# Half-query blocks at both ends of a gated attention kernel, with a new head, lighter norm rows and a gate row read in order

## The chip, the cores and the metric

The kernel runs on one core of one Trainium2 chip. The metric is the device time of one execution in microseconds. Each execution also reports its span, from the first to the last instruction (1.7 to 2.1 us less than the time here), and the mean clock that the throttle granted TensorE. All executions compared below are of the fast state; three timed ones (one each of after_vd2, after_strided and after_gap2: 423.23, 431.38 and 424.83 us) fell in the slow state, at a clock of 0.956 to 0.967, and are left out.

## The reference, cut to what matters

```python
x = A_x                                                # 1 x 2048 x 448, bf16
g = sigmoid((x * gate_w).sum(-1, keepdims=True))
q, k, v = split(x @ wqkv)                              # 16 heads of 28
a = softmax(q @ k.T * 28**-0.5) @ v @ wo               # per head, 2048 x 2048 scores
b = irfft2(rfft2(x) * (w_r + 1j * w_i))                # over both axes
return g * a + (1 - g) * b
```

The attention needs 16 x 2048 x 2048 exponentials. The Fourier part is done with matmuls between the attention's own.

## The kernel before

The 16 heads are four groups of four. A *score* is one 128x512 tile: 128 keys against 512 queries of one head. Four query blocks in each of four head groups make 16 blocks of work, each with 16 key tiles of four heads: 1024 scores in all. ScalarE takes most of the exponentials, two or three scores per instruction, from PSUM banks psA (3) and psB (2) to a ring in SBUF. For one to three key tiles of each block (the list ND) VectorE does it instead: it evicts the four scores as integers (y) and makes four phases from them (pd); each phase is multiplied with its own scaled copy of the values (vd), which GpSimd makes. TensorE sums the products of both kinds in the bank pvb.

These are the parts that the argument touches. `pool`, `dve`, `pe` and `act` do not issue an instruction: they hand an operation to a list scheduler with an assumed duration, dependences and a key, and the instructions are emitted in the order that it finds. Here GpSimd's scaling is assumed to take 0.6 us:

```python
            self.vdops[g] = []
            for f in range(4):
                def fp(f=f):
                    self.pin(nc.gpsimd.tensor_scalar(out=self.vd[:, f, :, :, 0:DH + 1], in0=self.vf[:],
                                                     scalar1=PHGAIN[f], scalar2=None, op0=ALU.mult))
                self.vdops[g].append(self.pool(0.6, fp, [e2, pw, self.vdms], due))
            self.vdready[g] = self.vdops[g][-1]
            ...
        for g in range(1, 4):                       # vd is one buffer: the old products must be done
            for o in self.vdops[g]:
                o.deps += self.vdlast.get(g - 1, [])
```

The keys of all operations are then moved by a list of some three thousand offsets (KOFF) that an earlier tuning found. Where the scheduler counts a busy share of TensorE below HAMF over the last HAMW = 3.4 us, it adds *filler* products of zeros.

The gate row of the Fourier part goes through DRAM, so that all partitions get it, and is read in steps of 16 elements:

```python
        d = self.dma(self.escr[:], self.ge[:], (m,), due + 20.0, dur=0.6, lat=4.0)      # escr is [P, NT]
        ...
                                                 in1=free_dims(self.erow[0:FN], [[0, 4], [NT, P]], g),
                                                 op=ALU.mult))
```

Of the kernel before, what the change touches and what calls it, by code (L numbers as in the profile page):

```python
# [23 lines left out]
UNITS = 512.0  # L24
# [23 lines left out]
def fft_consts():  # L48
# [45 lines left out]
    for ri, B in enumerate((Br, Bi)):  # L94
# [8 lines left out]
       "selc": (386, 192), "sel8": (578, 128), "selw": (706, 4)}  # L103
CSTN = 710
# [10 lines left out]
def small_consts():  # L115
# [10 lines left out]
    selc = np.zeros((P, 4, 48))  # L126
    for s in range(4):
        sv[32 * s:32 * s + 2] = 1.0
        selq[32 * s + 2:32 * s + 30, 32 * s] = -0.5
        selk[32 * s + 2:32 * s + 30, 32 * s + 1] = -0.5  # L130
        for b in range(4):
            selc[32 * s + 2:32 * s + 30, b, 16 + 4 * s + b] = -0.5
# [3 lines left out]
    put("selc", selc.reshape(P, 192))  # L136
# [25 lines left out]
class Item:  # L162
# [6 lines left out]
HAMW, HAMF = 3.4, 0.7421  # L169
DUE_P = 6.757  # L170
PVK, DUW, DFREE, WREL = 6.037, 11.4211, 1, 13.243
GK, GQ, GW, GV, GS, GREL = 6.918, 2.841, 7.618, 6.073, 2.662, 35.075
PROT, PTOL = 1.7838, 0.0685
FD = 2.303
EXT, XM, MPEN = 0, 0.0773, 4.0862
PDK = 1.0
PTN, PTD = 6, 20.0
KOFF = (
    (0, -3381), (1, -3445), (2, -3205), (3, -2978), (4, -2807), (5, -3003), (6, -2741), (7, -3070), (8, -2870),
    (9, -2933), (10, -2699), (11, -2432), (12, -2665), (13, -2889), (14, -2827), (15, -2875), (16, -3046),  # L180
    (17, -2813), (18, -2716), (19, -2526), (20, -2725), (21, -2957), (22, -2530), (23, -2791), (24, -2754),
    (25, -2847), (26, -2318), (27, -2163), (28, -2008), (29, -2195), (30, -1969), (31, -2290), (32, -2267),
    (33, -2067), (34, -2601), (35, -3137), (36, -3254), (37, -3031), (38, -3281), (39, -3296), (40, -2974),
    (41, -2802), (42, -2682), (43, -2539), (44, -2686), (45, -2183), (46, -2186), (47, -2367), (48, -2465),
    (49, -2217), (50, -2391), (51, -2580), (52, -2825), (53, -2743), (54, -2507), (55, -2843), (56, -2900),
    (57, -3179), (58, -3134), (59, -3379), (60, -3643), (61, -3140), (62, -3042), (63, -3134), (64, -2754),
    (65, -2650), (66, -2451), (67, -2565), (68, -2390), (69, -2220), (70, -2100), (71, -2159), (72, -2061),
    (73, -2085), (74, -2080), (75, -1960), (76, -1798), (77, -1549), (78, -1626), (79, -1557), (80, -1441),
    (81, -1328), (82, -2731), (83, -2587), (84, -2436), (85, -2518), (86, -2456), (87, -2507), (88, -2279),
    (89, -2452), (90, -2493), (91, -2144), (92, -1906), (93, -1954), (94, -2137), (95, -1875), (96, -1981),  # L190
    (97, -1911), (98, -1824), (99, -1714), (100, -1653), (101, -1305), (102, -1132), (103, -1215), (104, -1487),
    (105, -1438), (106, -1094), (107, -1077), (108, -1034), (109, -1025), (110, -1166), (111, -1450), (112, -1274),
    (113, -1191), (114, -1077), (115, -1190), (116, -1417), (117, -1541), (118, -1613), (119, -1649), (120, -1257),
    (121, -1226), (122, -1283), (123, -1151), (124, -1121), (125, -1455), (126, -1620), (127, -2002), (128, -1724),
    (129, -1720), (130, -1658), (131, -1595), (132, -1435), (133, -1466), (134, -1247), (135, -1465), (136, -1097),
    (137, -1198), (138, -1426), (139, -1342), (140, -1235), (141, -1526), (142, -1267), (143, -944), (144, -1058),
    (145, -1130), (146, -813), (147, -777), (148, -958), (149, -843), (150, -1414), (151, -1407), (152, -1433),
    (153, -1322), (154, -1705), (155, -1737), (156, -1657), (157, -1437), (158, -1254), (159, -1349), (160, -1242),
    (161, -1169), (162, -1495), (163, -1374), (164, -1386), (165, -1347), (166, -1379), (167, -1189), (168, -1306),
    (169, -1092), (170, -1354), (171, -1386), (172, -1548), (173, -1534), (174, -1628), (175, -1488), (176, -1507),  # L200
    (177, -1437), (178, -1344), (179, -1580), (180, -1276), (181, -1067), (182, -1143), (183, -1519), (184, -1575),
    (185, -1316), (186, -2323), (187, -2506), (188, -2184), (189, -2238), (190, -2117), (191, -1965), (192, -1937),
    (193, -2420), (194, -1921), (195, -1458), (196, -1355), (197, -1502), (198, -1355), (199, -1162), (200, -1029),
    (201, -1030), (202, -817), (203, -897), (204, -722), (205, -800), (206, -975), (207, -1152), (208, -1016),
    (209, -774), (210, -872), (211, -919), (212, -910), (213, -1000), (214, -892), (215, -809), (216, -728),
    (217, -844), (218, -806), (219, -644), (220, -533), (221, -950), (222, -650), (223, -1130), (224, -1204),
# [278 lines left out]
TA, TB = 43.678, 14.609  # L485
OUTD = 15
XREL = 9.034
SWP = 1.8725


class Sched:
# [60 lines left out]
    def run(self, nbg_tiles, dunits, dfree):  # L552
# [76 lines left out]
        def finish(o, t0, dur):  # L629
            nonlocal left  # L630
            if o.eng == "PE":
                pebusy.append((t0, t0 + dur))
                if o.name == "pv":
# [5 lines left out]
                    if o.last:  # L639
                        pvopen[1] = o.step  # L640
# [11 lines left out]
        while left:  # L652
            progress = False
            for e in engs:
# [3 lines left out]
                for o in pend[e]:  # L658
# [26 lines left out]
                    if best is None or k < best[0]:  # L685
                        best = (k, o)
# [60 lines left out]
class Kernel:  # L747
# [15 lines left out]
    def build(self):  # L763
# [8 lines left out]
        for o in order:  # L772
            o.emit()
# [1205 lines left out]
```

## Time and profile before

| | |
|---|---|
| time, median of three timed runs | 421.18 us (420.97 to 422.19) |
| time and span of the profiled execution | 424.53 us, 422.8 us |
| its mean clock | 0.992 |
| scores on ScalarE | 856, steps 1.33 us for three and 0.90 for two |
| first exponential starts, last ends | 12.07, 410.46 |
| holes between exponentials, summed step by step | 16.5 us |
| tail after the last exponential | 12.34 us |

The row to remember is the second: the trace is of an execution 3.3 us slower than the median. In the time-line lines further down the columns are start, duration, engine, source line, operation, tiles and count, and in brackets how long the engine sat idle before and what released it. One line also belongs here, the change from head group 0 to 1:

```profile
124.05 4.83 POOL L1362 TENSOR_SCALAR vd<-vf 128x348 bf16<-128x348 f32 x4 [9.85 <-PE pvb L868]
...
132.91 0.40 PE L868 MATMUL pvb<-pd,vd 128*32 128x512 bf16 x4
```

GpSimd waits for the old group's products, makes the new values until 128.88, and the first product that uses them comes at 132.91 without any wait: there are four microseconds to spare.

### The profile page before, as it was taken

The page shows a single profiled execution, that of the slowest core. Times are in us where ns is not written, and L with a number is a line of the kernel's source. Part 1 is how long each engine was busy: PE and PEld are TensorE (multiplying, and loading weights), DVE is VectorE, ACT ScalarE, POOL GpSimd, SP SyncE. Part 2 cuts the span into 40 slices and gives each one's busy share as a digit, 9 for nine tenths or more (in the row PEclk, how much of TensorE's full clock was granted, in tenths as well). Part 3 has the DMA queues.
Part 4 walks back from the last instruction along what each step waited for, and adds up shares of the span by engine and source line. Part 5 has one row for each costly group of instructions (what it writes and reads, how often), then busy time and mean ns, then how long its engine had stood idle before and what let it go on. Part 6 is the DMA issues. An engine that isn't in the chain of part 4 may idle for free.

```text
span 422.8 us, 12521 instructions
## 1 busy us (share of the span) xinstructions
PE 396.1 (94%) x5319; PEld 151.2 (36%) x5319; DVE 369.0 (87%) x670; ACT 396.1 (94%) x362; POOL 32.9 (8%) x63
## 2 busy tenths in 40 slices
PE   6899899999999999999999999999989999999986
PEld 4443232323443323334333323443333333333334
DVE  5658698967889999998999999999998989998883
ACT  4889899999999999999999999999997999999981
POOL 5310300000021000000004000000021000000000
PEclk9999899999999999999999999999998999999999
DMA  8400010001122310110110100213211300000011
GB/s 247 113 2 3 3 25 18 3 2 52 43 68 50 96 52 2 44 46 2 43 42 10 35 4 12 102 46 95 80 32 35 101 3 13 12 25 25 24 47 44
DMA packets 26348, 17.96 MB, mean 42 GB/s; under 512 B 10632, under 2 KB 24756, under 8 KB 26292
## 3 DMA queue, kind: packets, MB, share of 16 engines
q1 hardware_dynamic: 25524, 16.88, 14.6%
q8 instruction: 41, 0.67, 0.7%
q10 hardware_dynamic: 768, 0.28, 0.3%
q14 instruction: 15, 0.12, 0.1%
HBM read 11.27 MB, written 1.84 MB: 31 GB/s over the span
## 4 chain that ended last, share of the span: by engine, by line
PE 41%; ACT 29%; DVE 13%; issue 11%; DMA 3%; POOL 2%; ACTq 0%; DVEq 0%; POOLq 0%
ACT ring L1498 29%; PE bg L868 18%; PE pvb L868 11%; PE psA L868 6%; PE psB L868 6%; DVE y L1456 4%; DVE pd L1466 3%; DVE xtok L1919 3%; POOL vd L1362 2%; DMA xtok<-in_A_x_dram 1%; DMA U<-Y 1%; DMA U<-in_A_wqkv_dram 1%; PE bg L877 0%; DVE Y L1837 0%; DVE t L1879 0%
## 5 line engine op out<-in xcount | busy, mean ns | idle before, releaser
L1498 ACT ACTIVATE ring<-psA 128x1536 bf16<-128x1536 f32 (+1 forms) x172 | 264.2, 1536 | 8.8 <-PE psA L868 6.6
L1498 ACT ACTIVATE ring<-psB 128x1024 bf16<-128x1024 f32 x171 | 191.8, 1122 | 0.8 <-PE bg L868 0.5
L1456 DVE TENSOR_SCALAR y<-bg 128x512 uint16<-128x512 f32 x168 | 112.8, 686 | 14.1 <-PE bg L868 13.0
L1466 DVE TENSOR_SCALAR pd<-y 128x2048 uint16<-128x2048 uint16 x168 | 112.3, 687 | 0.5
L868 PEld LDWEIGHTS <-k 32*128 32x128 bf16 (+1 forms) x1088 | 44.6, 91 | 125.6 <-issue 120.6
L868 PE MATMUL pvb<-ring,vw 128*32 128x512 bf16 x856 | 78.6, 389 | 0.0
L868 PE MATMUL psA<-q,k 32*128 32x512 bf16 x514 | 68.2, 385 | 9.0 <-ACT ring L1498 8.1
L868 PE MATMUL psB<-q,k 32*128 32x512 bf16 x342 | 68.4, 384 | 2.0 <-ACT ring L1498 1.5
L868 PE MATMUL pvb<-pd,vd 128*32 128x512 bf16 x672 | 60.2, 385 | 4.2 <-POOL vd L1362 2.9
L868 PE MATMUL bg<-q,k 32*128 32x512 bf16 x168 | 62.7, 385 | 0.5 <-DVE xtok L1919 0.2
L868 PEld LDWEIGHTS <-vw 128*32 128x32 bf16 x856 | 20.5, 95 | 30.5 <-issue 26.9
L868 PEld LDWEIGHTS <-vd 128*32 128x32 bf16 x672 | 16.9, 95 | 28.6 <-issue 19.0
L1362 POOL TENSOR_SCALAR vd<-vf 128x348 bf16<-128x348 f32 x16 | 19.1, 1195 | 89.0 <-PE pvb L868 85.2
L868 PEld LDWEIGHTS <-xT 128*128 128x128 bf16 (+3 forms) x512 | 18.9, 96 | 13.4 <-issue 11.5
L1837 DVE CAST Y<-bg 128x450 bf16<-128x450 f32 x32 | 19.6, 619 | 1.8 <-PE bg L868 0.8
L868 PE MATMUL bg<-X,R 128*32 128x225 bf16 (+1 forms) x384 | 20.0, 294 | 0.2 <-DVE y L1456 0.2
L868 PE MATMUL bg<-xT,wpq 128*32 128x512 bf16 (+1 forms) x240 | 18.9, 395 | 0.3
L868 PE MATMUL bg<-xT,wpk 128*32 128x512 bf16 (+2 forms) x244 | 18.8, 381 | 0.1
L1919 DVE TENSOR_TENSOR xtok<-bg,xT 113x512 bf16<-113x512 f32 x16 | 16.3, 1028 | 2.9 <-PE bg L868 2.7
L868 PE MATMUL bg<-wo,q 128*32 128x448 bf16 x248 | 18.1, 356 | 0.6 <-DVE xtok L1919 0.4
L1879 DVE TENSOR_TENSOR t<-bg,Wg 128x900 bf16<-128x900 f32 x16 | 17.4, 1087 | 0.0
L868 PE MATMUL bg<-Bd,xtok 113*32 113x448 bf16 x256 | 17.2, 355 | 0.0
(118 smaller groups left out, 313.9 us busy)
## 6 DMA issues: line engine op xcount, KB each, us to landing
U<-Y SPq DMA_DIRECT2D x32, 112.5 KB
CR<-cRB SPq DMA_DIRECT2D x8, 256.0 KB
xtok<-in_A_x_dram SPq DMA_DIRECT2D x4, 448.0 KB
out_dram<-fin SPq DMA_DIRECT2D x14, 112.0 KB
CR<-cCS SPq DMA_DIRECT2D x8, 192.0 KB
xT<-escr SPq DMA_DIRECT2D x2, 512.0 KB
Wg<-in_B_w_i_dram SPq DMA_DIRECT2D x8, 112.5 KB
Wg<-in_B_w_r_dram SPq DMA_DIRECT2D x8, 112.5 KB
```

Of the source, the lines that this page charges most:

```text
L868: self.pin(self.nc.tensor.matmul(out, lhsT=lhsT, rhs=rhs, start=start, stop=stop, **kw))
L1362: self.pin(nc.gpsimd.tensor_scalar(out=self.vd[:, f, :, :, 0:DH + 1], in0=self.vf[:], scalar1=PHGAIN[f], scalar2=None, op0=ALU.mult))
L1456: self.pin(nc.vector.tensor_scalar(out=ys[:, s, :], in0=self.bgi(it), scalar1=127 * UNITS, scalar2=0.0, op0=ALU.add, op1=ALU.max))
L1466: self.pin(nc.vector.tensor_scalar(out=fl(pds).bitcast(U16), in0=fl(ys), scalar1=float(PHASE[f]), scalar2=0.25, op0=ALU.add, op1=ALU.mult))
L1498: self.pin(nc.scalar.activation(out=self.ring[:, u0:u0 + len(st), :], in_=slot[:, 0:len(st), :], func=ACT.Exp, scale=LN2 / UNITS))
L1837: self.pin(nc.vector.tensor_copy(out=y[:], in_=self.bgi(it)[:, 0:F2]))
L1879: self.pin(nc.vector.tensor_tensor(out=t4[:].rearrange("p (a b) f -> p a b f", a=2), in0=free_dims(self.bgi(it), [[0, 2], [F, 2], [1, F]]) ...
L1919: self.pin(nc.vector.tensor_tensor(out=self.ZT[0:FN, g, :].rearrange("p (a b) -> p a b", a=4), in0=self.bgi(it)[0:FN, :].rearrange("p (a b ...
```

## The change

The intent is to shorten both ends and to close holes. The first two key tiles of the first query block and four key tiles of the last are processed as half-queries of 256 columns, so that scores start when half a query is ready, and the first half's output can be worked off before the last exponential. The head loads tokens in two halves and shares the weight copies with ScalarE. The norm rows come from two passes over four column tiles instead of eight matmuls in series, and the key weights from the norm rows directly. The gate row is stored transposed. One more key tile goes to VectorE. All key offsets are new, and so are some ten other constants of the scheduler. The core of the diff, with cuts:

```diff
-HAMW, HAMF = 3.4, 0.7421
+HAMW, HAMF = 3.4, 0.735
 KOFF = ( ... all of the some three thousand offsets differ ... )
-    ND = [1, 2, 2, 3, 2, 3, 3, 3, 2, 3, 3, 3, 3, 3, 3, 3]
+    ND = [1, 2, 3, 3, 2, 3, 3, 3, 2, 3, 3, 3, 3, 3, 3, 3]
+            if n == 0:
+                ak = [("h", 0, 0, 1), ("h", 1, 0, 1)] + ak[2:]
+            if n == 15:
+                m = 2 * THP
+                ak = ak[:-m] + [("h", h, ak[i], ak[i + 1]) for h in range(2) for i in range(len(ak) - m, len(ak), 2)]
 ...
-        self.d_x.append(self.dma(self.xtok[:, 0:4, 0:D], self.x[:, 0:4, :], (), K0, dur=0.44, lat=3.6))
+        self.d_x.append(self.dma(self.xtok[:, 0:2, 0:D], self.x[:, 0:2, :], (), K0, dur=0.44, lat=3.2))
 ...
-        for w, sq in (("k", self.sq), ("q", self.sq2)):
-            for b in range(4):
-                def f3(w=w, b=b, sq=sq, n=len(ms)):
-                    o = 48 * b + (16 if w == "k" else 0)
-                    self.mc(self.bgi(it)[0:32, :], self.c("selc")[:, o:o + 32], sq[:, 512 * b:512 * b + 512], n == 0, n == 7)
+        for w, sq, lo in (("k", self.sq, 0), ("q", self.sq2, 32)):
+            def f3(w=w, sq=sq, lo=lo):
+                for b in range(4):
+                    self.mm(self.bgi(it)[32 * b:32 * b + 32, :], self.c("seln")[:, lo:lo + 32],
+                            sq[:, 512 * b:512 * b + 512], w == "k", w == "q", tile_position=(0, 32 * b))
 ...
-        d = self.dma(self.escr[:], self.ge[:], (m,), due + 20.0, dur=0.6, lat=4.0)
+        tt = self.dve(0.15, lambda: self.pin(nc.vector.transpose(out=self.get[:], in_=self.ge32[:])), (m, self.gms), due)
+        d = [self.dma(self.escr[:, 32 * i:32 * i + 32], self.get[32 * i:32 * i + 16, :], (tt,), due + 20.0, dur=0.6, lat=4.0)
+             for i in range(4)]
 ...
-                                                 in1=free_dims(self.erow[0:FN], [[0, 4], [NT, P]], g),
+                                                 in1=free_dims(self.erow[0:FN], [[0, 4], [1, P]], P * g),
```

Nothing in the diff's named parts concerns GpSimd's scaled values.

## The prediction

> **What bounds the kernel now.** I read the page first. ScalarE and TensorE are both busy 94% of the span, VectorE 87%, so the question is which of them sets the pace, and where. The two ScalarE groups (exponentials of scores, PSUM to the ring) are the largest, and ScalarE's own list of waits says what stops them:
>
> ```profile
> L1498 ACT ACTIVATE ring<-psA 128x1536 bf16<-128x1536 f32 (+1 forms) x172 | 264.2, 1536 | 8.8 <-PE psA L868 6.6
> L1498 ACT ACTIVATE ring<-psB 128x1024 bf16<-128x1024 f32 x171 | 191.8, 1122 | 0.8 <-PE bg L868 0.5
> L1919 DVE TENSOR_TENSOR xtok<-bg,xT 113x512 bf16<-113x512 f32 x16 | 16.3, 1028 | 2.9 <-PE bg L868 2.7
> ```
>
> The two groups sum to 456 us in a span of 422.8, because successive ones overlap, so I take steps between starts. In ScalarE's timeline a 3-score step is followed after 1.33 us and a 2-score step after 0.90 to 0.91 us (the medians): 2.235 us for five scores of 128x512, 0.447 us a score. There are 856 of them (1024 less 4 heads times the 42 key tiles that VectorE takes), 382.6 us. The first exponential starts at 12.07 and the last ends at 410.46: 398.4 us. So the span is head 12.07, pure exponentials 382.6, holes between them 15.8, tail 12.34. Only these four terms can change the time. By stage:
>
> ```profile
> 0.00:12.07 12.07, 8.20 (x64) 5.44 (x64) 6.38 (x14) 4.61 (x9) 5.56 (x21) 1.00 0.87 249
> 12.07:60.00 47.93, 44.38 (x561) 18.55 (x560) 34.89 (x64) 43.88 (x43) 9.68 (x22) 0.96 0.08 20
> 60.00:300.00 240.00, 230.69 (x3104) 86.06 (x3096) 222.94 (x418) 239.65 (x217) 12.61 (x16) 1.00 0.15 40
> 300.00:345.00 45.00, 40.12 (x567) 14.45 (x563) 40.31 (x62) 41.39 (x36) 5.08 (x4) 0.96 0.19 52
> 410.46:422.80 12.34, 8.30 (x136) 5.01 (x128) 5.35 (x12) 1.27 (x2) 0.00 (x0) 1.00 0.18 58
> ```
>
> Columns: stretch, length, busy us of PE, weight load, VectorE, ScalarE, GpSimd, clock, DMA share, GB/s. ScalarE is full from 60 to 300 (239.65 of 240) and lacks 4.05 us in 12 to 60 and 3.6 us in 300 to 345. Adding up late starts of exponentials step by step, I find 5.5 us lost before 60, 4.4 from 60 to 300, 5.7 from 300 to 345 and 0.9 after: 16.5, the 15.8 above within my rounding of the step. The worst holes:
>
> ```profile
> 27.92 1.45 ACT L1498 ACTIVATE ring<-psA 128x1536 bf16<-128x1536 f32 x1 [1.58 <-PE psA L868]
> 47.90 1.45 ACT L1498 ACTIVATE ring<-psA 128x1536 bf16<-128x1536 f32 x1 [1.49 <-PE bg L868]
> 316.51 0.40 PE L868 MATMUL pvb<-pd,vd 128*32 128x512 bf16 x4 [0.89 <-POOL vd L1362]
> 318.87 1.45 ACT L1498 ACTIVATE ring<-psA 128x1536 bf16<-128x1536 f32 x1 [1.64 <-PE psA L868]
> ```
>
> The first waits for the third key block (its norm matmul and VectorE's addition stand just before it). The second and the last have one cause: the value product of a VectorE tile waits for GpSimd's scaled values (four of 1.08 us each), and TensorE, in order, issues no scores meanwhile.
>
> Head and tail:
>
> ```profile
> 11.08 0.62 PE L877 MATMUL bg<-cst,xtok 128*128 128x128 bf16 x8 [1.48 <-DMA xtok<-in_A_x_dram]
> 11.64 0.39 PE L868 MATMUL psA<-q,k 32*128 32x512 bf16 x3
> ...
> 415.13 0.42 DVE L1684 TENSOR_TENSOR q<-pvs,psB 128x256 bf16<-128x256 f32 x1
> ...
> 418.06 0.94 PE L868 MATMUL bg<-Bd,xtok 113*32 113x448 bf16 x16
> ...
> 419.25 0.63 ACT L1706 ACTIVATE fin<-bg,gs 128x448 bf16<-128x448 f32 x1 [1.07 <-PE bg L868]
> ```
>
> The query was complete at 10.40, but the scores stood behind transposes whose tokens landed at 11.08. In the tail the last normalised query is ready at 415.55, but the last evacuation starts 3.7 us later: TensorE still accumulates whole output tiles.
>
> [...] the product of line 1919 reads its 4-byte second operand in steps of 64 bytes and takes 1.03 us, while the product of line 1610, of the same width and contiguous, takes 0.68. [...] 16 column-tiled projections at 14.81 take 1.05 us together, and one such matmul 0.38.
>
> **The change part by part.** The file does not hold an order of instructions but a list scheduler; I read the order it gives from the built program and count time in scores (0.447 us each).
>
> *Fewer exponentials.* Query block 2 now gives three key tiles to VectorE instead of two: 852 scores, so 4 x 0.447 = 1.8 us less on ScalarE, which is full there. VectorE pays four evictions and four phases of 0.69 us, 5.5 us, between about 58 and 82, where the slices show it 80 to 90% busy.
>
> *Head.* Tokens load as two halves, only the first half-query (256 columns) is projected before the first scores, and the weight copies are shared with ScalarE. I rebuild the chain from durations before. The first token load is half as large: I guess transposes at 4.1 instead of 4.48. ScalarE's table load (1.28) now follows its first weight load, so it ends at about 4.6; weight copies, the dummy exponential and one token copy bring ScalarE to 6.2. Projections of 256 columns end at 6.6 (key) and 6.9 (query), against 7.5 and 8.4. Key scaling and square (0.48 + 0.29), norm matmul (0.27) and ScalarE's copy (0.48), then the scores: exponential at about 9.5. The next 4 scores last 1.8 us; the second half-query's must then be ready. Their chain runs behind eight transposes of the second token block, which in the old kernel landed at 11.08; its load is now issued seventh on its queue, and I guess 9.5 to 10.5. The fifth score's exponential then starts at about 11.8. In the old kernel the fifth score's place is 12.07 + 1.8 = 13.86. Gain 2.1 (1 to 2.8).
>
> *Holes before 60.* The order asks for the third key block's norm by score 24 instead of 30, and needs it at 32: the hole at 27.92 should go. The last value block comes at score 49 instead of 58, and the four value products of the first VectorE tile are spread over scores 69, 72, 74, 77 instead of all at 70, so GpSimd's 4 x 1.08 us has time: the hole at 47.90 should go. Transposes of half the token blocks go to the value bank, free until the first value product. I expect 5.5 to become 2.5: gain 3.
>
> *Holes from 300 to 345.* The gate row is now stored transposed, so line 1919's product reads contiguously: 0.69 instead of 1.03, 14 of 16 in this stretch, 4.8 us of VectorE's 40.3. At the change to the last head group the first VectorE value product comes 10 scores (4.5 us) after the last of the group before, instead of 5 (2.2 us), against the 4.3 us that GpSimd needs. I expect 5.7 to become 2.2: gain 3.5.
>
> *Norm rows and key weights.* Eight matmuls in series on one column tile (0.21 us each, 1.7) become two passes over four tiles (about 0.5), three times: 3.6 us of TensorE. Sixteen key-weight matmuls of a 128-column weight become 4 x 4 small ones and no longer wait for the row's transfer. TensorE was waiting on others there; I count nothing by itself. The norm transfers go from 6 to 24 on the SyncE queue, each some 0.3 us of issue; they are wanted many microseconds later.
>
> *Tail.* The last block's final four key tiles are processed as half-queries, so the first half's products, reciprocals and output tiles run under the last exponentials, and after the end only two output tiles of one matmul step each remain. From the last exponential's end: products 0.5, addition of the second half 0.42, selection 0.6, reciprocal 0.21, broadcast 0.8 (eight narrow fp32 matmuls; the two old ones took 0.6 to 0.7, and the copy of 0.29 before them is gone), product 0.42, output matmuls 0.5, then two VectorE evictions of 0.68 in series or ScalarE's 0.63: 4.8. The last transfer is issued and lands in about 2.9 (old: eviction ends 419.88, span 422.80). Sum 7.7, against 12.34; I allow 0.3 for collisions with the first half. Gain 4.3.
>
> Sum: 1.8 + 2.1 + 3.0 + 3.5 + 4.3 = 14.7. Holes tend to reappear, since ScalarE, TensorE and VectorE are all near full and the whole order is new; I take off 1.5. 421.2 - 13.2 = 408.0 us.
>
> **Rivals.** (a) *VectorE or TensorE becomes the bound and the holes move instead of closing.* For it: VectorE stays near 90%, and the extra tile adds to it; against: the strided product gives back the same 5.5 us, and TensorE loses work. Then only head, tail and the 1.8 count: 8.2, so 413. (b) *The head gains nothing because a load lands late.* For it: the old kernel's transposes waited until 11.08 for tokens issued at 3.16, and the new queue puts value weights ahead of them; the wv weights are even fourteenth. Against: less is outstanding early. Then 410 to 411. (c) *The tail is hidden only in part*: the order interleaves first-half evictions of 0.68 with the second half's reciprocal and product on VectorE. Then 409.5. (d) *The clock falls*[...]; the stages stand at 0.96 to 1.00 now, and filler matmuls remain (46 groups of four against 37). Unlikely.
>
> **Range and chances.** The line of 2% is 421.18 x 0.98 = 412.8. The sure parts (fewer scores, tail) give 6; holes and head are needed for the rest, and (a) with (b) together end above the line. On the other side, if nearly all holes close, 404 is possible. Range 403.5 to 413; chances 0.84 faster, 0.15 the same, 0.01 slower.
>
> **What would show it.** In the new profile: 852 scores with steps still 1.33 and 0.90; the fifth score's exponential at 11 to 12.8; no wait of 1 us or more at the third key block or for GpSimd's scaled values; contiguous gate products near 0.69; the last exponential's end within 7 to 9 us of the end. I am wrong if VectorE or GpSimd opens new holes in 58 to 300, where there were only 4.4 us, or if the first scores wait for a token load.

## The result, and the profile after

The changed kernel took 417.80 us (median of four, 415.26 to 418.38), against 421.69 for the kernel before in the same session: a ratio of 0.990 (95% interval 0.985 to 0.994), so the same within 2%. Ratios here and below are the mean time of one kernel's fast runs over that of the other's fast runs of the same rounds, so they are not quite the ratio of the medians quoted. The prediction was 408.0 with a range to 413.0 and 84% on faster by over 2%. It was wrong by 9.8 us.

First the groups (columns: line, engine, operation, count, then busy us, mean ns, and idle time before with its releasers):

```profile
L1581 ACT ACTIVATE ring<-psA 128x1536 bf16<-128x1536 f32 x171 | 265.7, 1554 | 3.3 <-PE psA L881 2.4 <-PE psB L881 0.4 <-PE pvb L881 0.2
...
L881 PE MATMUL pvb<-pd,vd 128*32 128x512 bf16 x688 | 63.8, 386 | 3.2 <-POOL vd L1439 2.8 <-DVE pvs L1693 0.2
...
L2003 DVE TENSOR_TENSOR xtok<-bg,xT 113x512 bf16<-113x512 f32 x16 | 10.6, 684 | 1.2 <-PE bg L881 1.1
```

The gate product fell from 1028 to 684 ns as expected. The exponentials' steps are unchanged, 1.33 and 0.90 us. The values' products have one large wait, 2.8 us for GpSimd. By stage (columns as in the prediction):

```profile
9.83:60.00 50.17, 47.24 (x634) 20.61 (x633) 37.60 (x70) 48.35 (x47) 10.68 (x26) 1.00 0.17 45
60.00:120.00 60.00, 58.86 (x803) 21.00 (x799) 54.76 (x107) 60.00 (x56) 1.77 (x4) 1.00 0.07 15
120.00:140.00 20.00, 17.16 (x249) 6.26 (x246) 14.93 (x29) 14.80 (x14) 5.10 (x4) 0.83 0.27 70
140.00:300.00 160.00, 151.40 (x2034) 56.64 (x2026) 156.52 (x295) 158.65 (x143) 6.63 (x8) 0.99 0.16 43
300.00:345.00 45.00, 42.12 (x669) 16.94 (x669) 42.40 (x72) 45.00 (x41) 5.34 (x4) 1.00 0.20 55
405.90:415.20 9.30, 5.92 (x132) 4.00 (x132) 4.25 (x10) 0.63 (x1) 0.00 (x0) 1.00 0.24 76
...
127.40:134.00 6.60, 6.31 (x64) 1.99 (x64) 2.56 (x5) 2.48 (x2) 0.23 (x1) 0.50 0.15 38
```

ScalarE (the fourth busy figure) is now full from 300 to 345, where it lacked 3.6 us before, and lacks only 1.8 us up to 60. But from 120 to 140 it has 14.80 of 20 us. The kernel before, in the same stretch:

```profile
120.00:140.00 20.00, 19.59 (x284) 7.70 (x280) 19.86 (x40) 20.00 (x20) 4.62 (x4) 1.00 0.31 79
```

There ScalarE was full. So a hole of over 5 us has opened where none was. This is how it looks in the time-line of the changed kernel:

```profile
122.35 5.29 POOL L1439 TENSOR_SCALAR vd<-vf 128x348 bf16<-128x348 f32 x4 [17.27 <-PE pvb L881]
...
124.95 1.60 ACT L1581 ACTIVATE ring<-psA 128x1536 bf16<-128x1536 f32 x1
...
127.69 0.62 PE L881 MATMUL pvb<-pd,vd 128*32 128x512 bf16 x4 [2.83 <-POOL vd L1439]
...
130.12 1.02 ACT L1581 ACTIVATE ring<-psB 128x1024 bf16<-128x1024 f32 x1 [3.57 <-PE psB L881]
...
131.97 1.45 ACT L1581 ACTIVATE ring<-psA 128x1536 bf16<-128x1536 f32 x1 [0.82 <-PE psA L881]
...
134.22 1.02 ACT L1581 ACTIVATE ring<-psB 128x1024 bf16<-128x1024 f32 x1 [0.80 <-PE bg L881]
```

GpSimd waits 17.27 us for the last products of head group 0, then needs 5.29 us for its four scalings and ends at 127.64. TensorE, in order, stands 2.83 us at the first product of group 1, which starts 0.05 us later; no scores are issued meanwhile, so ScalarE stands too, 3.57 us. And then, from 127.4 to 134.0, the granted clock is 0.50 (the last line of the table by stage): the product takes 0.62 us instead of 0.40, and two more exponentials come late. By the step count the three holes are 3.84, 0.95 and 0.92 us, 5.7 together.

The head and the tail of the changed kernel:

```profile
9.83 1.45 ACT L1581 ACTIVATE ring<-psA 128x1536 bf16<-128x1536 f32 x1 [0.42 <-PE psB L881]
...
12.25 1.45 ACT L1581 ACTIVATE ring<-psA 128x1536 bf16<-128x1536 f32 x1 [0.48 <-PE psA L881]
...
18.40 1.45 ACT L1581 ACTIVATE ring<-psA 128x1536 bf16<-128x1536 f32 x1 [1.12 <-PE psA L881]
...
404.75 0.69 DVE L1723 COPY pvs<-pvb 128x512 f32<-128x512 f32 x1 [0.97 <-PE pvb L881]
...
406.88 0.61 PE L881 MATMUL bg<-sq,rr 128*32 128x128 f32 x16
...
407.32 0.61 PE L881 MATMUL pvb<-ring,vw 128*32 128x256 bf16 x16
...
408.04 0.41 DVE L1725 TENSOR_TENSOR pvs<-pvs,pvb 128x256 f32<-128x256 f32 x1
...
411.34 0.68 DVE L1789 SCALAR_TENSOR_TENSOR t<-psA,gs,X 128x448 bf16<-128x448 f32 x1
```

The first exponential starts at 9.83 instead of 12.07, and the fifth score's at 12.25. The hole at the third key block (27.92 before) is gone, but at 18.40 ScalarE now waits 1.12 us for the first scores of the *second* one, whose norm and VectorE addition end at 17.92. This hole, 1.25 us by the step count, is in every profile of the new order and the largest one that is left up to 60. The last exponential ends at 405.90, yet the last value products wait until 407.32, because TensorE first stands behind the first half's chain (copy, row sums, reciprocal, broadcast at 406.88). The tail is 9.30 us.

In spans: the head gave 2.2 us (12.07 to 9.83), the scores 1.8, the tail 3.0, and the holes only 0.7 (16.5 to 15.8 by the step count), together 7.7 against the measured 7.6 (422.8 to 415.2). By stage the holes moved as follows:

| stretch | before | changed |
|---|---|---|
| up to 60 | 5.5 | 3.0 |
| 60 to 120 | 1.3 | 0.9 |
| 120 to 140 | 0.4 | 5.9 |
| 140 to 300 | 2.6 | 3.8 |
| 300 to 360 | 5.7 | 1.6 |

Within 140 to 300 the changed kernel's new loss is one hole of 1.36 us at 198.95, again in a half-clock period (195.4 to 198.8).

### The profile page after: what moved, and what is told of

The parts are those of the page before. It is cut to its first block, busy times and chain, and to the rows that moved or that the text cites. A ratio compares the mean times of both kernels' runs of the same rounds, so it can differ in the third digit from the quotient of the medians.

```text
span 415.2 us, 12809 instructions
## 1 busy us (share of the span) xinstructions
PE 389.6 (94%) x5441; PEld 150.7 (36%) x5441; DVE 369.5 (89%) x681; ACT 391.9 (94%) x359; POOL 34.0 (8%) x64
## 4 chain that ended last, share of the span: by engine, by line
PE 40%; ACT 35%; DVE 12%; issue 8%; POOL 1%; DMA 1%; ACTq 0%; DVEq 0%; POOLq 0%
ACT ring L1581 35%; PE bg L881 17%; PE pvb L881 11%; PE psA L881 7%; PE psB L881 5%; DVE y L1535 3%; DVE pd L1545 2%; POOL vd L1439 1%; DMA U<-in_A_wqkv_dram 1%; DVE t L1963 1%; DVE k L1276 1%; DVE Y L1921 1%; PE bg L890 0%; DVE q L1276 0%; DVE pvs L1693 0%
## 5 line engine op out<-in xcount | busy, mean ns | idle before, releaser
L1581 ACT ACTIVATE ring<-psA 128x1536 bf16<-128x1536 f32 x171 | 265.7, 1554 | 3.3 <-PE psA L881 2.4
L1581 ACT ACTIVATE ring<-psB 128x1024 bf16<-128x1024 f32 (+1 forms) x170 | 191.9, 1129 | 5.8 <-PE psB L881 5.0
L1535 DVE TENSOR_SCALAR y<-bg 128x512 uint16<-128x512 f32 x172 | 114.6, 683 | 9.2 <-PE bg L881 8.7
L1545 DVE TENSOR_SCALAR pd<-y 128x2048 uint16<-128x2048 uint16 x172 | 115.2, 689 | 0.6
L881 PEld LDWEIGHTS <-k 32*128 32x128 bf16 (+1 forms) x1064 | 41.4, 91 | 127.8 <-issue 122.1
L881 PE MATMUL pvb<-ring,vw 128*32 128x512 bf16 (+1 forms) x876 | 79.5, 385 | 0.4 <-ACT ring L1581 0.3
L881 PE MATMUL psA<-q,k 32*128 32x512 bf16 (+1 forms) x529 | 67.7, 378 | 8.6 <-ACT ring L1581 6.9
L881 PE MATMUL psB<-q,k 32*128 32x512 bf16 (+1 forms) x347 | 66.8, 382 | 2.1 <-ACT ring L1581 1.4
L881 PE MATMUL pvb<-pd,vd 128*32 128x512 bf16 x688 | 63.8, 386 | 3.2 <-POOL vd L1439 2.8
L881 PE MATMUL bg<-Bd,xT 128*32 128x450 bf16 (+1 forms) x256 | 17.4, 356 | 0.0
```

Source lines behind the costliest of these rows:

```text
L881: self.pin(self.nc.tensor.matmul(out, lhsT=lhsT, rhs=rhs, start=start, stop=stop, **kw))
L1535: self.pin(nc.vector.tensor_scalar(out=ys[:, s, :], in0=self.bgi(it), scalar1=127 * UNITS, scalar2=0.0, op0=ALU.add, op1=ALU.max))
L1545: self.pin(nc.vector.tensor_scalar(out=fl(pds).bitcast(U16), in0=fl(ys), scalar1=float(PHASE[f]), scalar2=0.25, op0=ALU.add, op1=ALU.mult))
L1581: self.pin(nc.scalar.activation(out=self.ring[:, u0:u0 + len(st), :], in_=slot[:, 0:len(st), :], func=ACT.Exp, scale=LN2 / UNITS))
```

## The experiments

My theory was, in two parts: *the wait* (the new order leaves 8 scores instead of 18 between the last value product of head group 0 that uses GpSimd's values and the first of group 1, so TensorE waits there) and *the clock* (TensorE's idle time there brings half-clock periods; 19 of 44 timed runs of the kernel before had a clock of 1.000, of the changed kernel none of ten). The rivals were that another engine bounds that stretch anyway, and that the lighter norm rows are to blame. A third question was whether the holes that I had counted in the trace of the kernel before were in its timed runs at all. All thirteen runs that were made are told. In each, five timed rounds ran beside the kernel before.

| run | median us (fast runs) | ratio to before | 95% | mean clocks |
|---|---|---|---|---|
| changed kernel, first session | 417.80 (415.26 to 418.38) | 0.990 | 0.985 to 0.994 | 0.988 to 0.996 |
| after_again | 416.46 (415.46 to 418.59) | 0.986 | 0.983 to 0.990 | 0.988 to 0.996 |
| after_vd2 | 413.28 (413.06 to 414.24) | 0.981 | 0.978 to 0.984 | 0.995 to 1.000 |
| before_vd2 | 421.84 (420.37 to 422.87) | 1.000 | 0.997 to 1.003 | 0.992 to 1.000 |
| after_busy | 415.88 (413.10 to 417.24) | 0.985 | 0.982 to 0.988 | 0.987 to 0.999 |
| after_tail | 415.40 (414.06 to 416.87) | 0.985 | 0.982 to 0.988 | 0.986 to 0.996 |
| best | 412.30 (411.00 to 413.66) | 0.975 | 0.972 to 0.978 | 0.996 to 1.000 |
| best_fill | 434.02 (433.37 to 437.09) | 1.029 | 1.025 to 1.033 | 0.984 to 0.992 |
| after_strided | 421.08 (420.40 to 422.49) | 0.997 | 0.994 to 1.000 | 0.984 to 0.996 |
| after_gap (wrong result) | 411.57 (410.42 to 412.13) | 0.974 | 0.970 to 0.977 | 0.999 to 1.000 |
| after_norm | 417.94 (417.04 to 420.61) | 0.990 | 0.986 to 0.994 | 0.992 to 1.000 |
| before_again | 423.42 (422.85 to 424.35) | 1.003 | 0.999 to 1.006 | 0.988 to 0.996 |
| after_gap2 | 411.69 (410.79 to 412.40) | 0.974 | 0.970 to 0.978 | 0.996 to 1.000 |
| best_gap | 410.66 (409.86 to 411.36) | 0.971 | 0.968 to 0.975 | 0.999 to 1.000 |

### after_vd2: values of their own for head groups 1 and 3

GpSimd writes the values of group 1 to token memory that is dead by then, and those of group 3 to dead weight tiles; so it never waits for the old products. The order of all instructions is the same; the edit also adds five clearing instructions on GpSimd.

```diff
-                    self.pin(nc.gpsimd.tensor_scalar(out=self.vd[:, f, :, :, 0:DH + 1], in0=self.vf[:],
+                    self.pin(nc.gpsimd.tensor_scalar(out=self.vdout(g, f), in0=self.vf[:],
 ...
-                                lw = self.vd[:, f[0], v - (NT - DKT), s, :]
+                                lw = self.vdin(g, f[0], v - (NT - DKT), s)
```

> The changed kernel, in which GpSimd's scaled values of head groups 1 and 3 go to memory of their own (dead space), so that GpSimd no longer waits for TensorE's last products of the group before; the order of all instructions stays. Theory of the wait (the change from head group 0 to 1 was planned with 8 scores between the last old and the first new value product, 3.6 us, but GpSimd needs 4 x 1.1 to 1.6 us): the hole of ScalarE's exponentials between 124.95 and 134.2 (5.7 us by the step count) and the half clock from 127.4 to 134.0 go, and the time falls by 4 to 6 us to 412 to 414, a ratio of about 0.976 to 0.98 to the kernel before, against 0.990. Rival (VectorE or TensorE bounds that stretch anyway): the hole moves to a later exponential before 150 and the time falls by less than 1.5 us.

```profile
115.40 5.05 POOL L1464 TENSOR_SCALAR xtok<-vf 128x348 bf16<-128x348 f32 x4 [9.61 <-DVE ge L1475]
...
125.95 0.40 PE L904 MATMUL pvb<-pd,xtok 128*32 128x512 bf16 x4
```

GpSimd is done at 120.45, the first new product at 125.95 waits for nothing, and ScalarE is busy 19.86 of the 20 us from 120 to 140. The ratio went from 0.990 and 0.986 (two sessions) to 0.981, 2 to 4 us, and the hole of 5.7 us is gone from the trace. In this profile a half-clock period turned up at 151 instead and took 1.4 us in two late exponentials. The theory of the wait holds, though the gain is below the 4 to 6 us that I expected. The rival falls by the trace, which has no new hole of over 0.5 us before 150; by the times alone it would be close, since this interval touches that of after_again.

### before_vd2: the same buffers in the kernel before

The edit is the same, in the kernel before.

> The kernel before with the same two buffers. Its own wait for GpSimd at a change of group is the one at 316.5 (0.89 us, then 1.64 us at 318.87, and half clock from 317.1 to 321). If the trace of before, whose own execution was 3.3 us longer than the median of the timed runs, shows what the timed runs have, the time falls by 3 to 4 us (ratio 0.991 to 0.993). Rival (the profiled execution was an unlucky one, and the holes that I budgeted for this stage are smaller in timed runs): the ratio is 0.996 to 1.000, and the 3.5 us that the prediction counted for this stage were never all there to win.

The ratio is 1.000. In the trace the wait at 316 is gone: the holes from 300 to 340 fell from 5.2 to 3.1 us, and ScalarE is busy 43.37 us of 300 to 345 instead of 41.39. But the holes from 40 to 60 were 4.3 us instead of 2.9 in this execution, with a half clock from 46 to 53. The timed runs suggest why that is no gain. Here are the 44 timed runs of the kernel before that ran beside the experiments, sorted by their clock:

| mean clock | runs | time, us |
|---|---|---|
| 1.000 | 19 | 420.9 to 422.0, mean 421.2 |
| 0.996 | 11 | 422.2 to 423.8, mean 422.7 |
| 0.992 | 7 | 422.9 to 424.3, mean 423.5 |
| 0.987 or 0.988 | 7 | 424.3 to 425.8, mean 425.0 |

A half-clock period in the traces lasts 3.4 us (in the profile of before, the slices of 1 us from 48 on have 0.56, 0.50, 0.50 and 0.73, so 1.7 us of clock are lost) or twice that (46.1 to 52.9 in before_vd2); 1.7 of 422 us is 0.004, the distance of these rows. So the runs seem to differ by how many such stretches of 3.4 us they have, none to three, and each goes with 0.8 to 1.5 us more. This is a correlation over runs; no run here changes the clock alone. The trace that I predicted from, at 0.992, had two of them, at 48 and at 317, in the very stages whose holes I meant to close. At equal clocks before_vd2 is about 1 us faster (420.4 at 1.000 against 421.2; two runs at 0.992, 422.5 against 423.5), but only one of its six runs was at 1.000, where eight of eleven were for the kernel before in that session. Whether that is chance is open. The rival holds: 3 to 4 us were not there to win.

### after_busy: idle products while TensorE waits

```diff
+                    if kind == "d" and g == 1 and not hasattr(self, "busy"):
+                        self.busy = True
+                        for r in range(24):
+                            self.filler(-1 if o.first else None, 256)
```

> The changed kernel with 24 idle products of zero weights (256 columns, four column tiles, about 0.11 us each, 2.6 us in all) on TensorE just ahead of the first product of a VectorE tile in head group 1, where it stands idle for 2.8 us. Theory of the clock (the half clock after 127.4 follows from TensorE's idle time there, as it does in the kernel before after 46 and 316): the first hole of 3.8 us stays, the clock stays at 1.00 after it, and the holes at 130.12 and 131.97 (1.9 us together) go: 1.5 to 2.5 us less time, ratio 0.984 to 0.987. Rival (the clock falls for another reason, or the later holes come from the order and not the clock): half clock and the holes stay, ratio 0.989 to 0.991.

```profile
126.33 2.81 PE L881 MATMUL pvb<-zero 128*32 128x256 bf16 x96
126.51 1.60 ACT L1581 ACTIVATE ring<-psA 128x1536 bf16<-128x1536 f32 x1
129.27 0.40 PE L881 MATMUL pvb<-pd,vd 128*32 128x512 bf16 x4
130.69 1.02 ACT L1581 ACTIVATE ring<-psB 128x1024 bf16<-128x1024 f32 x1 [2.58 <-PE psB L881]
131.73 1.45 ACT L1581 ACTIVATE ring<-psA 128x1536 bf16<-128x1536 f32 x1
```

The idle products fill the wait; it is there all the same and ScalarE still stands, 2.58 us. But the clock after it stays at 1.00, the product takes 0.40, and the next exponential follows without a hole: the holes from 120 to 140 are 3.2 us instead of 5.9. So in the traces the half clock goes with TensorE's idle time here: 0.50 from 127.4 to 134.0 after the empty wait of 2.83 us, 1.00 from 127 to 134 with the wait filled. The timed ratio of 0.985 lies where the theory put it, but its interval overlaps that of the changed kernel in both sessions, so the time alone would not show it. The profile also has a half-clock period from 194.2 to 197.6 with a hole of 1.36 us, as the changed kernel's first profile had at 195.4.

### after_tail: the broadcast behind the last products

```diff
-                m.append(self.pe(0, fb, [r] + m[-1:], -89.0 + h, dur=0.24, mode="col"))
+                m.append(self.pe(0, fb, [r] + m[-1:] + (last if h == 0 else []), -89.0 + h, dur=0.24, mode="col"))
```

The dependence also moves some of VectorE's and TensorE's work of the last 10 us.

> The changed kernel with one more dependence in the last block: the broadcast of the first half-query's reciprocals is issued after the last value products and not before them. Theory of the tail (the last products ran 1.4 us after the last exponential because TensorE, in order, stood behind the first half's chain of VectorE copy, reciprocal and broadcast): the tail after the last exponential falls from 9.3 to about 8.1 us, the time by 1 to 1.3 us, ratio about 0.987. Rival (VectorE's evictions of the first half's output tiles set the end, and they get later by as much): tail 9 to 9.5 us, ratio 0.989 to 0.991.

```profile
405.10 0.61 PE L881 MATMUL pvb<-ring,vw 128*32 128x256 bf16 x16
...
405.92 0.41 DVE L1725 TENSOR_TENSOR pvs<-pvs,pvb 128x256 f32<-128x256 f32 x1
...
410.74 0.40 SPq L863 DMA_DIRECT2D out_dram<-fin  x1
```

The last exponential ends at 404.76 here, the products run 0.34 us later instead of 1.4, and the second half's addition at 405.92. The tail is 8.74 us (413.5 less 404.76), against 9.30 and, in after_again, 9.98. What now comes last is an output tile of the *first* half, issued at 410.74: its eviction stands on VectorE behind the second half's. So both the theory and its rival are in part right: 0.6 to 1.2 us were won in the trace, and the first half's evictions took the rest. At equal clocks (0.994 to 0.996) the runs average 415.3 us against 415.9 for the changed kernel.

### after_again and before_again: the kernels themselves

> The changed kernel once more, for a second profile and five more times beside the other runs. Theory of the clock (each half-clock period of TensorE, about 3.4 us, costs some 1 to 2 us and comes or goes from run to run, except that the idle 2.8 us at the change to head group 1 brings it on nearly always): median 415 to 418.5, ratio 0.986 to 0.993, mean clocks of 0.988 to 0.996 and hardly ever 1.000; the hole at 125 is there again, the one at 196.3 may be absent. Rival (what I saw at 196.3 comes from the lighter norm rows and key weights of the change): both are there again, at the same places.

> The kernel before itself, five more times and with a second profile. Its timed runs show mean clocks of 1.000 (421.1 to 422.0 us), 0.992 to 0.996 (422 to 424) and 0.988 (424 to 426); the profile that I predicted from was of a run at 0.992 (424.5). If the profiled run has a higher clock this time, the holes at 48 to 52 and 317 to 321 are shorter and their sum is nearer to 13 than to 16.5; if it has the same clock, they are there again. Ratio 0.998 to 1.002.

The second profile of the changed kernel has the hole at 125 again (3.78 us, then 0.62) with half clock from 127 to 131, but none at 196: the same instructions ran at full clock there. None of the ten timed runs of the changed kernel in two sessions reached a clock of 1.000. The period at 127 is in both profiles of the changed kernel, while that at 196 comes and goes: after_busy and after_strided have it again (from 194.2 and 196.2), after_tail and after_norm do not. Of the kernel before, I hoped for a profile at a higher clock and did not get one: it ran at 0.988, with half clock from 45 to 52 and from 318 to 322, and holes of 17.4 us in all. A trace of it at a clock of 1.000 was never taken; that its holes are smaller there is inferred from the times.

The repeated profiles also show how far the head varies. In the kernel before, the first exponential starts at 12.07 in the profile that I predicted from, but at 10.89 in before_again and 10.91 in before_vd2: the wait of 1.48 us for tokens at 11.08 is in the first alone. Twelve profiles have the head of the changed kernel. Seven of them start at 9.79 to 10.00, five (after_gap, after_strided, best, after_busy, after_tail) at 10.69 to 11.46. In these five TensorE's matmuls run slower in part of the stretch from 5 to 11 us; for instance the same four projections in the changed kernel and in after_busy:

```profile
7.36 0.60 PE L881 MATMUL pvb<-xT,wpk 128*128 128x256 bf16 x4
...
8.02 1.06 PE L881 MATMUL pvb<-xT,wpk 128*128 128x256 bf16 x4
```

The clock records in the traces fit: the first record of full clock comes at 4.2 to 4.8 us in the other seven (4.28 in the changed kernel's first), but at 8.45 to 9.94 in four of the five, and in best the clock is at half again from 7.4 to 10.8. What the clock was before the first record is not shown; the mean clocks quoted here count it as full. On average of the profiles the new head starts 0.9 us earlier than the old one (10.4 against 11.3), not 2.2.

### after_strided: the gate row in steps of 64 bytes again

```diff
-        d = [self.dma(self.escr[:, 32 * i:32 * i + 32], self.get[32 * i:32 * i + 16, :], (tt,), due + 20.0, dur=0.6, lat=4.0)
+        d = [self.dma(self.escr[32 * i:32 * i + 32, :], self.ge[32 * i:32 * i + 32, :], (tt,), due + 20.0, dur=0.6, lat=4.0)
 ...
-                                                 in1=free_dims(self.erow[0:FN], [[0, 4], [1, P]], P * g),
+                                                 in1=free_dims(self.erow[0:FN], [[0, 4], [NT, P]], g),
```

> The changed kernel with the gate row stored as in the kernel before, so that the 16 gate products of VectorE read their second operand in steps of 64 bytes again; the order stays. Each product takes 1.03 us instead of 0.69, 14 of them in 300 to 345: 4.8 us of VectorE there. Theory (the contiguous read closed the holes of 300 to 345): 2 to 3 us of holes come back there, ratio 0.995 to 0.997 where the changed kernel has 0.990. Rival (VectorE has room there in the new order, and the order or the clock closed the holes): less than 1 us comes back.

```profile
300.00:345.00 45.00, 41.40 (x636) 16.37 (x632) 43.26 (x67) 42.70 (x38) 5.43 (x4) 0.96 0.19 56
```

ScalarE loses 2.3 us of that stretch again, the clock in it is 0.96 (half from 326 to 330), and the holes from 300 to 360 are 5.5 us instead of 1.6. The ratio is 0.997 where after_again in the same session has 0.986: 0.0107 of 422, 4.5 us; against the first session's 0.990 it is 3.0 us. The theory holds and the rival (less than 1 us) falls. The contiguous read is thus worth 3.0 to 4.5 us, of the size of the 4.8 us by which it relieves VectorE there (14 products of 1.028 us in the trace of before and 0.684 in the changed kernel's). It is the largest part that was taken out alone; most others were not.

### after_norm: heavier norm rows

```diff
+                for r in range(7 if w == "k" else 1):
+                    for b in range(4):
                         self.mm(self.bgi(it)[32 * b:32 * b + 32, :], self.c("seln")[:, lo:lo + 32],
-                            sq[:, 512 * b:512 * b + 512], w == "k", w == "q", tile_position=(0, 32 * b))
+                                sq[:, 512 * b:512 * b + 512], w == "k", w == "q" or r < 6, tile_position=(0, 32 * b))
```

> The changed kernel with the first of the two passes of the norm matmuls done seven times over (same result), three times in the kernel: 6 x 0.2 to 0.25 us, about 1.3 to 1.5 us of TensorE each, a little more than what the new form of the norm rows saves (1.2 us each). The prediction counted nothing for that saving. Theory: time as the changed kernel, ratio 0.986 to 0.991. Rival (TensorE is full enough for it to count): 1.5 us for each of three, ratio 0.994 to 1.000.

The time is as the changed kernel's in the first session and 1.7 us longer (0.990 against 0.986) than in the second; the intervals overlap, so it is inconclusive. The trace has a hole at each of the three places, at 102.46, 192.28 and 254.37 (1.05, 0.86 and 0.92 us), where the second profile of the changed kernel has none over 0.25. Yet three of its six runs were at a clock of 1.000, which the changed kernel never reached, though this trace still has the half clock at 127. What I counted as nothing may thus be worth two to three microseconds on its own, in part paid back by a steadier clock. Neither is shown by the times.

### best, and best_fill

best puts after_vd2 and after_tail together. best_fill adds more filler products, by one number:

```diff
-HAMW, HAMF = 3.4, 0.735
+HAMW, HAMF = 3.4, 0.745
```

> The changed kernel with both edits: memory of their own for GpSimd's scaled values of head groups 1 and 3, and the first half-query's broadcast behind the last value products. If the two effects are independent (3.8 us for the values by the ratios 0.9897 and 0.9806; 0.6 us for the tail, whose length fell from 9.30 to 8.74 in the trace), 412.5 to 413.5 us, ratio 0.979 to 0.981, and a mean clock of 1.000 in most runs. Rival (the hole moves elsewhere with another phase of the clock): 414 to 416.

> The same as the run called best, with the scheduler's target for idle filler products of TensorE raised from 0.735 to 0.745 (157 groups of four instead of about 40; this alters the order in many places). If half-clock periods still cost time in best, they go and the time falls by up to 1 us with a clock of 1.000 in all runs. Rival (fillers stand in front of useful work and the new order is not the tuned one): the clock is 1.000 but the time is 1 to 4 us longer than best.

best is at 412.3 us, ratio 0.975 (0.979 to 0.981 expected): the two effects add up, within the interval. best_fill is a failure for another reason than the clock. The altered number changed the order. Up to about 260 us the holes are as in best, but then ScalarE stands 4.54 us until 300 and 12.64 us until 359. In the second wait VectorE is busy 11.65 of the 12.60 us and TensorE 11.40; I take it for a backlog of evictions that the tuned offsets had kept away, but did not trace it. The number of fillers can't be varied alone in this kernel, so this run says nothing about fillers.

### after_gap, wrong, and after_gap2: the order alone

These two leave the memory as it is and let more scores stand between the old and the new products. after_gap told the scheduler a longer duration:

```diff
-                self.vdops[g].append(self.pool(0.6, fp, [e2, pw, self.vdms], due))
+                self.vdops[g].append(self.pool(5.0 if g == 1 else 0.6, fp, [e2, pw, self.vdms], due))
```

> The changed kernel with one number altered: the scheduler is told that each of GpSimd's four scalings for head group 1 takes 5.0 us instead of 0.6. That moves only the order of TensorE's work around the change of group: 15 scores stand between the last value product of group 0 and the first of group 1, instead of 8 (18 in the kernel before); all other engines keep their order and no memory is added. Theory of the wait: 7 scores more are 3.1 us more of ScalarE's work ahead of the wait, so the wait of 2.8 us for GpSimd is all but gone, the hole of 3.8 us at 125 falls to under 1, no half clock follows, and the time falls by 3 to 4.5 us: ratio 0.977 to 0.981. Rival (the later products hold up VectorE's six result buffers and so open the hole elsewhere): less than 1.5 us is won, ratio over 0.983.

It gave a wrong result, with a relative error of 0.045, and I had not meant it to. The scheduler takes a product to depend on the *last listed* of the four scalings only, but runs them in the order of their keys. With 0.6 us all four were over before the first product; with 5.0 some of them were emitted behind products that should have read them, which then read the old group's values. (The text below says three; the trace shows two that start, at 129.92 and 134.36, after the first new product at 129.20.) Its time is no evidence, since it also waited for less. The mended run states a duration as the trace has it, and the missing dependence:

```diff
-                self.vdops[g].append(self.pool(0.6, fp, [e2, pw, self.vdms], due))
+                self.vdops[g].append(self.pool(1.25 if g == 1 else 0.6, fp, [e2, pw, self.vdms], due))
-                    deps += [self.pdops[n, kt, f[0]][0], self.vdready[g]]
+                    deps += [self.pdops[n, kt, f[0]][0], self.vdready[g]] + (self.vdops[g] if g == 1 else [])
```

> The run after_gap mended: the scheduler is told 1.25 us for each of GpSimd's four scalings of head group 1 (the trace has 1.1 to 1.6) instead of 0.6, and that each value product of that group depends on all four; in after_gap the longer time alone let three of the scalings be issued behind products that should have read them, hence its wrong result, and hence it waited for less than it should. Now 15 scores stand between the last product of group 0 and the first of group 1 (8 in the changed kernel, 18 before), all products read the right values, and only TensorE's order differs. Theory of the wait: the hole of 3.8 us at 125 falls to under 1, no half clock follows, clocks of 1.000 in most runs, 411 to 413.5 us, ratio 0.974 to 0.980. Rival (after_gap was fast only because it did not wait): the wait for GpSimd is still there at 1 us or more, 414 to 416.5, ratio 0.983 to 0.988.

```profile
122.48 5.19 POOL L1439 TENSOR_SCALAR vd<-vf 128x348 bf16<-128x348 f32 x4 [17.28 <-PE pvb L881]
...
128.47 0.61 PE L881 MATMUL pvb<-pd,vd 128*32 128x512 bf16 x8
```

GpSimd is as late as ever, done at 127.67, but the first product now comes at 128.47 and waits for nothing. ScalarE is busy 20.00 of the 20 us from 120 to 140, no half clock occurs before the end of the kernel, and the holes sum to 9.0 us. The result is right, the time 411.69 us (median of five fast runs), ratio 0.974. By the ratios that is 5.1 to 6.6 us less than the changed kernel (0.986 and 0.990). Only TensorE's order around one place differs. The theory of the wait is shown: either another order of these products or more memory (after_vd2) removes it, so the order alone is enough.

### best_gap: the version that beats both

The edits of after_gap2 and after_tail, three lines in all.

> The edits of after_gap2 and of after_tail together, three lines altered in the changed kernel. If both are worth what they were alone: 410.5 to 412 us, ratio 0.972 to 0.976, tail 8.7 us in the trace, clock 1.000 in nearly all runs. Rival (another phase of the clock or of the tail takes it back): as after_gap2.

It takes 410.66 us, ratio 0.971 (0.968 to 0.975), with a right result: 2.9% faster than the kernel before, and the fastest of all right ones. The tail in its trace is 8.71 us (408.0 less 399.29), and its clocks are 0.999 or 1.000 in all six runs.

## Why the prediction was wrong

**The step that failed first is "Holes from 300 to 345"**, where I judged one change of head group, the last, and wrote that there the first product comes "10 scores (4.5 us) after the last of the group before, instead of 5 (2.2 us), against the 4.3 us that GpSimd needs". That closed the wait, though with nothing to spare: the four scalings took more than the 4.3 us assumed (the trace that I read has 5.3 us there, from 313.90 to 319.20), and in the changed kernel the first new product starts at 315.23, 0.02 us after GpSimd ends. It came out because the first scaling had run at 305.57 already; the other three take 4.1 us together, and a fourth would not have fitted. But the same comparison at the change from group 0 to 1 gives 8 scores instead of 18, 3.6 us against GpSimd's 5.29, and I did not make it. In the built order it was there to read. The holes from 60 to 300, which the sum left at 4.4 us with 1.5 for new ones, became 10.6. What it cost is the difference between the changed kernel (median 416.9 us of ten runs in two sessions) and after_gap2 (411.7), 5.2 us. Rival (a), that holes move instead of closing, happened, though by a wait for GpSimd and not by VectorE or TensorE being full.

**The second is the last line of the sum, "421.2 - 13.2 = 408.0".** The gains were counted in a trace of an execution of 424.5 us, and subtracted from the median of others, 421.2. Of the 3.3 us between them, about 2.3 (421.2 to 423.5 in the table of 44 runs) go with the half-clock periods at 48 and 317, which sit in the two stages whose holes I closed on paper. The remaining 1 us fits the wait for tokens at 11.08, which made this head 1.2 us longer than that of the two other profiles. I took both off once in the median and once more in the sum. What speaks for this is the table, the heads, and before_vd2, which removed one of those holes in the trace and won nothing in the time; it is not shown by an experiment of its own. From the profiled execution the same sum gives 424.5 - 13.2 = 411.3; after_gap2, which has the change without the missed wait, took 411.7. That this is so near is partly luck, since a tail 1.3 us too long stands against 1.5 us set aside and not needed.

**The clock, rival (d), was called unlikely and happened.** In the changed kernel's trace the clock fell to half at 127.16, inside the wait of 2.83 us in which TensorE stood (124.86 to 127.69). Half clock came near 127 (129 in after_tail) in all five traces in which TensorE idled in this wait (the changed kernel's two, after_tail, after_strided and after_norm), and near 195 in three of the six profiles of this order (the changed kernel's first, after_busy, after_strided). I should have asked at each new wait of TensorE whether it brings one on. In the changed kernel's trace the times between changes of the clock are 122.88, 6.83, 61.44 and 3.41 us, all whole multiples of 3.41; what sets that grid is not shown. Of the 5.7 us at 125, 1.9 were this in the trace: the two later holes, which after_busy removed.

**The tail was mis-sized.** I expected 8.0 us and got 9.3 to 10.0. The terms after the last products were nearly right; the missing 1.4 us is that TensorE reaches them only at 407.32. Rival (c) named VectorE's evictions as the danger; it was TensorE's own order first, as after_tail shows, and then the evictions.

**What was right.** 852 scores with unchanged steps, 1.8 us. In the changed kernel's own profile the head: first exponential 9.83 (9.5 expected), fifth score 12.25 (11.8), no wait for a token load. Some of that is luck. The first transposes came at 5.00 and not at the guessed 4.1, after 0.74 us of waiting for the constants; the old head was a slow one; and in five of twelve profiles the new one was 0.7 us or more later. So rival (b) fell as to tokens, but most of the 2.1 us was not there against a usual old head. The holes up to 60 went from 5.5 to 3.0 where I had 2.5, though part of the 5.5 was half clock and 1.25 us of the 3.0 is the new wait at 18.40. The holes of 300 to 360 (the prediction says 345, but its 5.7 reach to 360) went from 5.7 to 1.6 where I had 2.2; the gate products fell to 0.684 us as worked out, and after_strided puts that part alone at 3.0 to 4.5 us, where I had 3.5 for the whole stage. (The 14 of 16 products in 300 to 345 are those of the new order; in the old trace 12 begin there.) That the norm rows count for nothing is not confirmed: the trace of after_norm speaks for a little more, the times leave it open.

The account closes: 408.0 predicted, plus 3.3 for the base, 5.2 for the missed wait and 1.3 for the tail is 417.8; the median measured over both sessions is 416.9. The rest of about 1 us is a residue that I did not trace further; I had set 1.5 aside for new holes, and in after_gap2 they were not needed (9.0 us of holes in all, against the 9.3 that the prediction's own steps leave of 15.8).

## What to carry to other kernels

When a change gives a new order, compare it at *every* instance of a hand-over (here all three changes of head group), not at the one that hurt in the old trace; the built order shows it before anything is run. Subtract gains from the execution in which they were counted, and look first at how that execution stands among the timed ones. And give a scheduler the durations and the dependences that the trace shows: two lines did here at least as much as two more buffers (0.974 against 0.981).

## What the traces show of the clock and of GpSimd

- In the changed kernel's trace TensorE was busy 2.85 of the 5.40 us from 122.0 to 127.4, with the wait of 2.83 us in it, and half clock followed, as in the four other traces in which it idled there. At 195.4 half clock followed a stretch in which TensorE was busy 3.22 of 4.00 us (191.6 to 195.6), with no gap over 0.3 us that the trace shows; in the second profile of the same program it did not. A busy share does not tell the cases apart: from 302.8 to 306.2 TensorE was busy 2.49 of 3.40 us, a smaller share, and the clock stayed at 1.00.
- In the 44 runs of the kernel before, sorted by mean clock, each 3.4 us of half clock goes with 0.8 to 1.5 us of 421. Their number, none to three by the mean clock, goes with most of the spread between its fast runs, so runs are best compared at equal mean clock.
- GpSimd's scaling of 128x348 from fp32 to bf16 took 1.08 us at the least and up to 1.59 (16 of them in the changed kernel's trace, median 1.09). What makes the difference was not tried; the measured figure is the one to plan with, not the 0.6 us that the scheduler was told.
